# Gate and up projections of a GEGLU block as pairs of 64-row half tiles, with the weights loaded in chunks of 64 rows

## Chip, core and metric

The kernel runs on one core of one Trainium2 chip. The metric is device time in microseconds (us), the median of three runs. Traces come from one more execution under the hardware profiler; its span, from the first to the last instruction, is a little shorter than its own time.

## What is computed

For x of 2048 tokens by 448 features, in bf16:

```python
xn = _layernorm(x)
out = x + attention(xn, wqkv, wo) + (gelu(xn @ w_gate) * (xn @ w_up)) @ w_down
# attention: 16 heads of 28, causal, each token sees itself and the 255 before it
# w_gate, w_up: 448 x 1792; w_down: 1792 x 448
```

## The kernel before

Tokens are worked in four blocks (`qb`) of 512. `xnT` holds the normalized x with features on the partitions: 448 features are three chunks of 128 and a rest of 64. The rest stands in chunk 3 twice, on partitions 0 to 63 and on 64 to 127, so that two 64-row matmuls can run side by side in the upper and lower half of the array.

TensorE (PE) executes in program order, and the program writes that order out by hand. A block has two stages.

`attention(qb, ...)` (from line 532) goes through score steps: 12 in block 0, 10 in the others. A step issues scores (line 616, tile shape 28 x 128 or 28 x 64), the exp on ScalarE (ACT, line 622) and, in some steps, PV (line 576). Between the steps, matmuls of other work are put in from a `Feed`, a queue of generators with a planned cost: `gen_qk` and `gen_v` (projections of this or the next block), `gen_up` (ups done early; three pairs in block 0, five in block 3) and `gen_down` (the output of the block before). A generator that yields `HOLD` has dense passes standing open, and its half passes are issued at the start of the next step.

`gated(qb, ...)` (lines 417 to 479) then computes gates and the ups that are left. There are 14 tiles of 128 FFN features, taken in pairs. Each output takes three dense passes of 128 rows (`three`, line 232 by the helper `mm3`) and one of 64 rows (`half`, line 238 by `mm_half`). The 64-row passes of several outputs are grouped, so that the array changes its tile shape less often: (0, 2), (4, 8, 6), (10, 12) in blocks 0 and 3, four groups in the others. ACT makes the gelu (line 464), VectorE (DVE) the product with the up (line 471, or 469 for an up done early). PV of the last four heads (`last_v`) stands behind the first group's halves. `hook` puts norms, transposes and the k3 copies of the next block in between.

PSUM has four banks for scores or gate pairs (`s`) and four more: `m` twice, `d` and `o`, given out by fixed tags.

Weights: `wu` and `wg` hold three chunks of 128 rows, each loaded by one DMA (lines 144 and 750). The rest of 64 rows is loaded to both halves, by tiles `wgu3` and `wug3` (lines 145, 146, 748, 749). All are issued from SyncE (SP): `wu` at the start, behind x and wqkv; `wg`, wo and wd in `loads()`, which `ahead3` calls in block 0's third step. x tiles 8 to 11 are loaded at line 147 (issued at 8.93 us), 12 to 15 at line 747 (22.96 us). `dma_transp` (line 217) transposes the normalized tiles 4 to 15 by DMA, also from SP. In block 0 the order of the feed is: projections of heads 4 to 15, two early ups, projections of block 1, one early up.

Of the kernel before, what the change touches and what calls it, by code (L numbers as in the profile page):

```python
# [8 lines left out]
ACT = mybir.ActivationFunctionType  # L9
# [7 lines left out]
P = 128  # L17
# [58 lines left out]
def kernel(  # L76
# [45 lines left out]
    def rows(w, c0, n):  # L122
        return w[c0 * P:(c0 + n) * P, :].rearrange("(c p) n -> p c n", p=P)

# [14 lines left out]

    ident = const.tile([P, P], bf16, name="ident")  # L140
# [3 lines left out]
    nc.sync.dma_start(out=wu[:, :, :], in_=rows(B_w_up, 0, 3))  # L144
# [36 lines left out]
    xnT = const.tile([P, 4, S], bf16, name="xnT")  # L181
    qT = const.tile([P, 4, S], bf16, name="qT")
# [59 lines left out]
    ring = [("m", "m", "d"), 0]  # L242

    def bank(name):

        tag = ring[0][ring[1] % len(ring[0])]
        ring[1] += 1
        return psum.tile([P, QB], f32, name=name, tag=tag, bufs=2 if tag == "m" else 1)
# [8 lines left out]
    def v_copy(t, pv, copy):  # L257
        copy(out=v_sb[:, t, :, 0:Dh], in_=pv.rearrange("p (h d) -> p h d", d=Dh))

    def gen_v(qb, ts):  # L260

        for t in ts:
            pvs = []
            for i in range(2):
                pvs.append(bank("pv")[:, 0:D])
# [17 lines left out]
    def qk_copies(qb, g, pq, pk):  # L283
        ts = slice(qb * QB, (qb + 1) * QB)
        nc.scalar.copy(out=qT[:, g, ts], in_=pq)
        nc.vector.tensor_copy(out=kT[:, g, ts], in_=pk)
        done.add((qb, g))

    def gen_qk(qb, gs, others=()):

        for g in gs:
            pq = bank("pq")[:, :]
            proj(pq, wqp, qb, g)
            if qb and g == 3:
# [4 lines left out]
                nc.scalar.copy(out=qT[:, 3, ts], in_=pq)  # L299
                done.add((qb, 3))  # L300
# [3 lines left out]
            pk = bank("pk")[:, :]  # L304
# [52 lines left out]
    UP1 = 1660  # L357
    STEP, PV = 450, 870

    hTs, oNs = {}, {}  # L360
    down_tag, last_tag, last_res = ["d"], [None], []

    def gen_down(qb, tags):

        hT, oN = hTs[qb], oNs[qb]
        for tt in range(4):
            t = 4 * qb + tt
            cs = slice(tt * P, (tt + 1) * P)
            for n, (lo, up) in enumerate(((0, D),) if t < NT - 1 else ((0, D // 2), (D // 2, D))):
                w = up - lo  # L370
                tag = tags[tt + n]
                down_tag[0] = tag
                po = psum.tile([P, QB], f32, name="po", tag=tag, bufs=2 if tag == "m" else 1)
# [11 lines left out]
                nc.vector.tensor_tensor(out=res[:, 0:w], in0=po[:, 0:w], in1=x_sb[:, t, lo:up], op=ALU.add)  # L385
                nc.sync.dma_start(out=outv[:, t, lo:up], in_=res[:, 0:w])
# [7 lines left out]
    def half(ps, f, gate, hi, ts, start, stop, m=P):  # L394

        w3 = wgu3 if gate != bool(hi) else wug3
        mm_half(ps, w3[:, f * P:(f + 1) * P], xnT[:, 3, ts], hi, start, stop, m)

    def three(ps, f, gate, ts, start, stop):
        w = wg if gate else wu  # L400
        mm3(ps, lambda c: w[:, c, f * P:(f + 1) * P], lambda c: xnT[:, c, ts], start, stop)

    def gen_up(qb, fs):

        ts = slice(qb * QB, (qb + 1) * QB)
        for f in fs:
            us = []
            for i in range(2):
                us.append(bank("ue"))
                three(us[i][:, :], f + i, False, ts, True, False)  # L410
                yield (650, HOLD) if i else 650
            for i in range(2):
                half(us[i][:, :], f + i, False, i, ts, False, True)
            for i in range(2):
                nc.vector.tensor_copy(out=hTs[qb][:, f + i, :], in_=us[i][:, :])  # L415
            yield -360

    def gated(qb, early, last_v, flush, hook):

        ts = slice(qb * QB, (qb + 1) * QB)  # L420
        hT = hTs[qb]
        turn = ["o" if down_tag[0] == "d" else "d", down_tag[0]] * 4

        def single(name, tag):
            return psum.tile([P, QB], f32, name=name, tag=tag, bufs=2 if tag == "m" else 1)[:, :]

        def begin(f, apart=False):
            last_tag[0] = turn[0] if f not in early else last_tag[0]
            pr = dict(f=f, us=[])
            if apart:  # L430
                pr["gs"] = [single("g0", tag) for tag in ("m", turn.pop(0))]
                return pr
            pr["gt"] = phase[0].pool.tile([P, 2, QB], f32, name="gt", tag="s")
            pr["gs"] = [pr["gt"][:, i, :] for i in range(2)]
            if f not in early:
                tags = ("m", turn.pop(0))
                if qb == 0 and f == 0:
                    tags = [ring[0][(ring[1] + i) % 3] for i in range(2)]
                    if "d" in tags:
                        turn.insert(0, "o")  # L440
                pr["us"] = [single("u0", tag) for tag in tags]
            return pr

        def dense(pr, start):
            f = pr["f"]
            gs = [(g, f + i, True) for i, g in enumerate(pr["gs"])]
            us = [(u, f + i, False) for i, u in enumerate(pr["us"])]
            for ps, fi, gate in (gs + us if f else us + gs):
                three(ps, fi, gate, ts, start, not start)

        def halves(pr, start, m):
            f = pr["f"]
            for i in range(2):
                if pr["us"]:
                    half(pr["gs"][i], f + i, True, 0, ts, start, not start, m)
                    half(pr["us"][i], f + i, False, 1, ts, start, not start, m)
                else:
                    half(pr["gs"][i], f + i, True, i, ts, start, not start, m)

        def end(pr):  # L460
            f = pr["f"]
            ge = work.tile([P, 2, QB], bf16, name="ge", bufs=2)
            if "gt" in pr:
                nc.scalar.activation(out=ge[:, :, :], in_=pr["gt"][:, :, :], func=ACT.Gelu_apprx_tanh)  # L464
            else:
                for i, g in enumerate(pr["gs"]):
                    nc.scalar.activation(out=ge[:, i, :], in_=g, func=ACT.Gelu_apprx_tanh)
            if not pr["us"]:
                nc.vector.tensor_tensor(out=hT[:, f:f + 2, :], in0=ge[:, :, :], in1=hT[:, f:f + 2, :], op=ALU.mult)
            for i, u in enumerate(pr["us"]):  # L470
                nc.vector.tensor_tensor(out=hT[:, f + i, :], in0=ge[:, i, :], in1=u, op=ALU.mult)  # L471
                flush()
            hook(f)

        for fs in ((0, 2), (4, 8, 6), (10, 12)) if qb in (0, 3) else ((0,), (2, 4), (6, 8), (10, 12)):
            prs = [begin(fs[0])]
            dense(prs[0], True)
            prs += [begin(f, len(fs) == 3 and f == fs[1]) for f in fs[1:]]
            for pr in prs:
                halves(pr, pr is not prs[0], 32 if qb and not fs[0] else P)  # L480
            if not fs[0]:
                last_v()
            end(prs[0])
            for pr in prs[1:]:
                dense(pr, False)
                end(pr)
# [49 lines left out]
    def attention(qb, feeds, aux, plan):  # L536
# [22 lines left out]
        def add_halves(oc, ov):  # L559
            nc.scalar.copy(out=oc[:, :], in_=ov[0][:, :])  # L560
            nc.vector.tensor_tensor(out=oc[:, :], in0=oc[:, :], in1=ov[1][:, :], op=ALU.add)  # L561

# [4 lines left out]
        def pv(g):  # L567

            tags = ("o",) if not qb else ("m", "m" if g < 3 else down_tag[0])
            ov = [psum.tile([P, QB], f32, name="ov", tag=tag, bufs=2 if tag == "m" else 1) for tag in tags]  # L570
            todo = parts.pop(g)
            for n, (half, kt, q0, nq, col, p_sb) in enumerate(todo):
                k0 = 64 * half if half else 0
                r = slice(k0, k0 + (P if half is None else 64))
                for j in range(4):
                    nc.tensor.matmul(ov[half or 0][32 * j:32 * j + 32, q0:q0 + nq], lhsT=v_sb[r, kt, 4 * g + j, :],  # L576
                                     rhs=p_sb[r, j, col:col + nq], start=n == (half or 0), stop=n + len(tags) >= len(todo),
                                     tile_position=(k0, 32 * j), skip_group_check=True)
            oc = work.tile([P, QB], f32, name="oc", tag="wb" if qb and g % 2 else "wa", bufs=1)
            if qb:  # L580
                if g == 2 or qb == NB - 1 and g == 3:
# [3 lines left out]
            else:  # L585
                nc.vector.tensor_copy(out=oc[:, :], in_=ov[0][:, :])
            copied.append((g, oc))

        if qb:
            feeds[0].run()  # L590
        steps = list(steps_of(qb))
        pvs = {4: 0, 6: 1, 9: 2} if qb else {4: 0, 7: 1, 10: 2}
        for i, (scores, ncol, edges) in enumerate(steps):
# [42 lines left out]
            else:  # L636
# [9 lines left out]
                share(feeds, want, to)  # L646
# [29 lines left out]
    def alone(name, tag):  # L676
        return psum.tile([P, QB], f32, name=name, tag=tag, bufs=1)[:, 0:D]

# [272 lines left out]
```

## Time and profile before

| | |
|---|---|
| median of 3 runs | 220.48 us (220.33 to 220.51) |
| profiled execution: its time | 221.15 us |
| profiled execution: span | 219.4 us |
| mean granted PE clock | 0.996 |
| DVE busy, ACT busy | 152.1 us, 133.3 us |
| 128-row passes of gates, ups and early ups (line 232) | 37.5 + 29.2 + 12.0 us in three groups |
| wu and wg, one DMA of 1,344 KB each | issued at 7.22 and 24.77 us |

The page gives busy times, and slices of the span in which a row of digits or of GB/s tells what went on when. In a group's line the numbers are busy time and mean length of one. Matmuls are pipelined: a pass of 512 columns is listed with 379 ns, and the next starts 216 ns after it. So starts are compared, not lengths. PEld is PE's loading of weights, which runs beside matmuls.

### The profile page before, as it was taken

To read this page: it belongs to the slowest core of one execution; us is meant where nothing else is said; L and a number is where in the kernel's file an instruction comes from. 1 tells how busy PE (TensorE), PEld (TensorE's weight loads), DVE (VectorE), ACT (ScalarE), POOL (GpSimd) and SP (SyncE) were. 2 spreads that over 40 slices of the span, in tenths; PEclk is the share of its full clock that TensorE was granted. 3 is DMA by queue.
4 is the path that set the end of the run, shared out by engine and by line. 5 is a ranking of instruction groups with operands and counts; after the bars stand their busy time and mean duration, and the time that the engine had idled before them with its cause. 6 is when DMAs were issued, how large, how long until landed. Compare 5 with 4: busy or idle time off the path is not lost.

```text
span 219.4 us, 5447 instructions
## 1 busy us (share of the span) xinstructions
PE 213.9 (98%) x2287; PEld 96.1 (44%) x2287; DVE 152.1 (69%) x346; ACT 133.3 (61%) x131; POOL 46.9 (21%) x80
## 2 busy tenths in 40 slices
PE   7999999999999999999999999999999999999993
PEld 2433333434444454444444445444344445444562
DVE  6787896799666883679565795386356799479521
ACT  3588788662878875432878888233486777565000
POOL 5377987320000120022000022022000022022001
PEclk9999999999999999999999999999999999999998
DMA  6993799104200001102300000200000000000011
GB/s 193 310 311 71 188 325 302 30 4 72 45 3 21 24 24 27 20 3 46 60 13 24 23 1 24 52 13 0 0 3 21 25 3 24 24 1 0 22 35 37
DMA packets 18045, 13.30 MB, mean 61 GB/s; under 512 B 8704, under 2 KB 16992, under 8 KB 18016
## 3 DMA queue, kind: packets, MB, share of 16 engines
q1 hardware_dynamic: 17072, 12.62, 21.1%
q8 instruction: 19, 0.31, 0.6%
q10 hardware_dynamic: 944, 0.29, 0.5%
q14 instruction: 10, 0.08, 0.1%
HBM read 9.15 MB, written 2.18 MB: 52 GB/s over the span
## 4 chain that ended last, share of the span: by engine, by line
PE 96%; ACT 1%; DVE 1%; issue 1%; DVEq 0%
PE po L380 20%; PE gt L232 16%; PE u L232 12%; PE sc L616 6%; PE po L375 6%; PE gt L238 5%; PE ue L232 5%; PE ov L576 5%; PE pq L232 4%; PE pv L232 4%; PE pk L232 3%; PE wps L191 2%; PE pq L238 1%; PE g L232 1%; PE ue L238 1%; PE pv L238 1%
## 5 line engine op out<-in xcount | busy, mean ns | idle before, releaser
L622 ACT ACTIVATE p_sb<-sc 128x2048 bf16<-128x2048 f32 (+2 forms) x42 | 73.8, 1758 | 12.6 <-PE sc L616 8.2
L380 PE MATMUL po<-wd,hT 128*128 128x448 bf16 (+1 forms) x238 | 49.8, 342 | 0.0
L464 ACT ACTIVATE ge<-gt 128x1024 bf16<-128x1024 f32 x26 | 26.6, 1024 | 34.9 <-PE u L238 20.1
L542 POOL TENSOR_TENSOR oN<-oc,l 128x512 bf16<-128x512 f32 x12 | 16.0, 1334 | 137.8 <-DVE l L556 87.4
L232 PE MATMUL gt<-xnT,wg 128*128 128x512 bf16 x156 | 37.5, 380 | 0.0
L471 DVE TENSOR_TENSOR hT<-ge,u 128x512 bf16<-128x512 bf16 x40 | 25.7, 682 | 12.9 <-ACT ge L464 12.9
L380 PEld LDWEIGHTS <-hT 128*128 128x128 bf16 x238 | 21.5, 98 | 18.8 <-issue 2.6
L232 PE MATMUL u<-xnT,wu 128*128 128x512 bf16 x120 | 29.2, 379 | 0.0
L523 DVE TENSOR_TENSOR p_sb<-p_sb,masks 128x256 bf16<-128x256 bf16 (+1 forms) x90 | 26.8, 353 | 0.4 <-ACT p_sb L622 0.4
L232 PEld LDWEIGHTS <-wg 128*128 128x128 bf16 x168 | 15.3, 98 | 21.3 <-issue 4.5
L232 PEld LDWEIGHTS <-wu 128*128 128x128 bf16 x168 | 16.0, 98 | 19.2 <-issue 1.0
L561 DVE TENSOR_TENSOR oc<-oc,ov 128x512 f32<-128x512 f32 x12 | 8.2, 687 | 16.5 <-ACT oc L560 16.5
L616 PE MATMUL sc<-qT,kT 28*64 28x320 bf16 (+7 forms) x640 | 16.9, 263 | 0.2
L415 DVE CAST hT<-ue 128x512 bf16<-128x512 f32 x16 | 10.2, 681 | 8.4 <-PE ue L238 8.3
L375 PE MATMUL po<-wo,oN 128*128 128x448 bf16 (+1 forms) x68 | 15.9, 343 | 0.0
L385 DVE TENSOR_TENSOR res<-po,x_sb 128x448 bf16<-128x448 f32 (+1 forms) x17 | 10.0, 586 | 8.6 <-PE po L380 8.4
L533 POOL TENSOR_SCALAR_AFFINE_SELECT p_sb<-p_sb 128x512 bf16<-128x512 bf16 (+1 forms) x20 | 14.2, 730 | 5.0 <-ACT p_sb L622 4.8
L238 PE MATMUL gt<-xnT,wgu 64*128 64x512 bf16 (+1 forms) x67 | 12.7, 380 | 0.0
L560 ACT COPY oc<-ov 128x512 f32<-128x512 f32 x12 | 7.0, 583 | 8.8 <-PE ov L576 8.8
L232 PE MATMUL pq<-xnT,wqp 128*128 128x512 bf16 x45 | 12.2, 380 | 0.1
L548 DVE STREAM_TRANSPOSE l<-oc 128x512 f32<-128x512 f32 x16 | 11.3, 704 | 1.4 <-POOL oN L542 1.2
L232 PE MATMUL ue<-xnT,wu 128*128 128x512 bf16 x48 | 12.0, 380 | 0.0
(97 smaller groups left out, 241.9 us busy)
## 6 DMA issues: line engine op xcount, KB each, us to landing
out_dram<-res SPq DMA_DIRECT2D x15, 112.0 KB
x_sb<-in_A_x_dram SPq DMA_DIRECT2D x3, 448.0 KB
wu<-in_B_w_up_dram SPq DMA_DIRECT2D x1, 1344.0 KB
wg<-in_B_w_gate_dram SPq DMA_DIRECT2D x1, 1344.0 KB
wd<-in_B_w_down_dram SPq DMA_DIRECT2D x3, 448.0 KB
wraw<-in_A_wqkv_dram SPq DMA_DIRECT2D x2, 252.0 KB
wo<-in_A_wo_dram SPq DMA_DIRECT2D x4, 98.0 KB
wv<-in_A_wqkv_dram SPq DMA_DIRECT2D x1, 336.0 KB
```

Of the source, the lines that this page charges most:

```text
L232: nc.tensor.matmul(ps, lhsT=lhs(c), rhs=rhs(c), start=start and c == 0, stop=stop and c == 2, skip_group_check=True)
L238: nc.tensor.matmul(ps[c:c + m], lhsT=lhs[p0:p0 + 64, c:c + m], rhs=rhs[p0:p0 + 64], start=start, stop=stop, tile_position=(p0, c), skip_gr ...
L375: nc.tensor.matmul(po[:, 0:w], lhsT=oN[:, g, cs], rhs=wo[:, g, lo:up], start=(g == 0), stop=False, skip_group_check=True)
L380: nc.tensor.matmul(po[:, 0:w], lhsT=hT[:, f, cs], rhs=wd[:, f, lo:up], start=False, stop=(f == NF - 1), skip_group_check=True)
L464: nc.scalar.activation(out=ge[:, :, :], in_=pr["gt"][:, :, :], func=ACT.Gelu_apprx_tanh)
L471: nc.vector.tensor_tensor(out=hT[:, f + i, :], in0=ge[:, i, :], in1=u, op=ALU.mult)
L523: nc.vector.tensor_tensor(out=reg, in0=reg, in1=m, op=ALU.mult)
L533: nc.gpsimd.affine_select(out=reg, in_=reg, pattern=mid + [[1 if diag else -1, min(w, P)]], compare_op=ALU.is_ge, fill=0.0, base=0 if diag ...
L542: nc.gpsimd.tensor_tensor(out=oN[:, g, :], in0=oc[:, :], in1=inv, op=ALU.mult)
L548: nc.vector.transpose(out=l1[:, :, :].rearrange("p a b -> p (a b)"), in_=oc[:, :])
L616: nc.tensor.matmul(ss[k0:k0 + nk, j, col:col + nq], lhsT=kT[r, g, kt * P + k0:kt * P + k0 + nk], rhs=qT[r, g, qb * QB + q0:qb * QB + q0 + ...
L622: nc.scalar.activation(out=p_sb[:, :, 0:ncol], in_=ss[:, :, 0:ncol], func=ACT.Exp, scale=SCALE)
```

## The change

All 448 rows of gate and up are cut in seven chunks of 64 (`c`). Partitions 0 to 63 of `wu` and `wg` hold a chunk's columns for FFN tiles 0 to 6, partitions 64 to 127 those for tiles 7 to 13. One pair `p` is the tiles p and p + 7: seven passes of 64 rows for each, side by side in the two halves of the array, into two PSUM banks. Each half needs all seven x chunks on its own partitions. Half of them stand there in `xnT`; for the others `xsw`, a copy of the block's three full chunks with the halves exchanged, is made by two DMAs (`swap`), in block 0 from ACT's queue, later from SP's at the start of the attention.

`wu` and `wg` are loaded by seven DMAs each (`load_ffn`), one per chunk. `wgu3` and `wug3` go. x tiles 8 to 11 are loaded in `loads()`, ahead of 12 to 15. The fixed PSUM tags give way to a list of four free banks: `take` hands out the one free longest, `give` puts it back where its last reader is issued. `gated` has no groups any more. The feed of block 0 mixes ups and projections, and the attention no longer starts with a run of `feeds[0]`.

```diff
-    wg = const.tile([P, 3, F], bf16, name="wg")
-    wu = const.tile([P, 3, F], bf16, name="wu")
-    wgu3 = const.tile([P, F], bf16, name="wgu3")
-    wug3 = const.tile([P, F], bf16, name="wug3")
+    wg = const.tile([P, 7, F // 2], bf16, name="wg")
+    wu = const.tile([P, 7, F // 2], bf16, name="wu")
...
+    def load_ffn(dst, w):
+        for c in range(7):
+            nc.sync.dma_start(out=dst[:, c, :], in_=w[64 * c:64 * c + 64, :].rearrange("p (h n) -> h p n", h=2))
...
+    load_ffn(wu, B_w_up)
...
-    nc.sync.dma_start(out=wu[:, :, :], in_=rows(B_w_up, 0, 3))
-    nc.sync.dma_start(out=wug3[0:64, :], in_=B_w_up[384:448, :])
-    nc.sync.dma_start(out=wgu3[64:128, :], in_=B_w_up[384:448, :])
-    nc.sync.dma_start(out=x_sb[:, 8:12, :], in_=xv[:, 8:12, :])
...
+    spare = ["b0", "b1", "b2", "b3"]
+    held = {}
+
+    def take(name, cols=QB, tag=None):
+        tag = tag or spare[0]
+        spare.remove(tag)
+        ps = psum.tile([P, QB], f32, name=name, tag=tag, bufs=1)[:, 0:cols]
+        held[id(ps)] = tag, ps
+        return ps
+
+    def give(*tiles):
+        for ps in tiles:
+            spare.append(held.pop(id(ps))[0])
...
+    def swap(qb, queue):
         ts = slice(qb * QB, (qb + 1) * QB)
+        for hi in range(2):
+            queue.dma_start(out=xsw[64 * hi:64 * hi + 64, :, :], in_=xnT[64 - 64 * hi:P - 64 * hi, 0:3, ts])
+
+    def chunk(pair, w, p, qb, c):
+        for hi, ps in enumerate(pair):
+            r = slice(64 * hi, 64 * hi + 64)
+            ts = slice(qb * QB, (qb + 1) * QB)
+            x = xnT[r, 3, ts] if c == 6 else xnT[r, c // 2, ts] if c % 2 == hi else xsw[r, c // 2, :]
+            nc.tensor.matmul(ps, lhsT=w[r, c, p * P:(p + 1) * P], rhs=x, start=c == 0, stop=c == 6,
+                             tile_position=(64 * hi, 0), skip_group_check=True)
...
+    def gen_up(qb, ps):
+        for p in ps:
+            us = [take("ue") for _ in range(2)]
+            for c in range(7):
+                chunk(us, wu, p, qb, c)
+                if c == 2:
+                    yield 640
+                if c == 5:
+                    yield 640, HOLD
...
+        up(0)
+        gate(0)
+        end(0)
+        gate(1)
...
+        for p in range(3, 7):
+            gate(p)
+            up(p)
+            end(p)
...
-                if g == 2 or qb == NB - 1 and g == 3:
+                if g > 1:
                     behind.append((oc, ov))
...
-        if qb:
-            feeds[0].run()
...
+                if qb == NB - 1:
+                    share(feeds[:1], want, 0)
+                    share(feeds, 0, to)
+                else:
+                    share(feeds, want, to)
...
     transp(3, nc.vector.tensor_copy, "b3")
+    swap(0, nc.scalar)
...
     def loads():
-        nc.sync.dma_start(out=x_sb[:, 12:16, :], in_=xv[:, 12:16, :])
-        nc.sync.dma_start(out=wgu3[0:64, :], in_=B_w_gate[384:448, :])
-        nc.sync.dma_start(out=wug3[64:128, :], in_=B_w_gate[384:448, :])
-        nc.sync.dma_start(out=wg[:, :, :], in_=rows(B_w_gate, 0, 3))
+        for t in (8, 12):
+            nc.sync.dma_start(out=x_sb[:, t:t + 4, :], in_=xv[:, t:t + 4, :])
+        load_ffn(wg, B_w_gate)
...
-            early = (2, 4, 8)
+            early = (1, 2, 4)
             feeds = [Feed((gen_qk(0, (1, 2, 3), [(t, pvs[t]) for t in (2, 3)]), 3 * QK1 + 360),
-                          (gen_up(0, (2, 8)), 2 * UP1), (gen_proj(1), PROJ), (gen_up(0, (4,)), UP1))]
+                          (gen_up(0, (1,)), UP1), (gen_v(1, (4,)), 1500), (gen_up(0, (4,)), UP1), (gen_v(1, (6,)), 1500),
+                          (gen_up(0, (2,)), UP1), (gen_qk(1, range(4)), PROJ - 3000))]
...
+        if qb:
+            swap(qb, nc.sync)
```

More of the change, by code (lines that the diff above doesn't have):

```diff
@@ L181 @@
     xnT = const.tile([P, 4, S], bf16, name="xnT")
+    xsw = const.tile([P, 3, QB], bf16, name="xsw")
     qT = const.tile([P, 4, S], bf16, name="qT")
@@ L258, in v_copy @@
         copy(out=v_sb[:, t, :, 0:Dh], in_=pv.rearrange("p (h d) -> p h d", d=Dh))
+        give(pv)
     def gen_v(qb, ts):
@@ L264, in gen_v @@
             for i in range(2):
-                pvs.append(bank("pv")[:, 0:D])
+                pvs.append(take("pv", D))
                 v_dense(t + i, pvs[i])
@@ L286, in qk_copies @@
         nc.vector.tensor_copy(out=kT[:, g, ts], in_=pk)
+        if not (qb == 0 and g == 0):
+            give(pq, pk)
         done.add((qb, g))
@@ L291, in gen_qk @@
         for g in gs:
-            pq = bank("pq")[:, :]
+            pq = take("pq")
             proj(pq, wqp, qb, g)
@@ L299, in gen_qk @@
                 nc.scalar.copy(out=qT[:, 3, ts], in_=pq)
+                give(pq)
                 done.add((qb, 3))
@@ L303, in gen_qk @@
             yield 650
-            pk = bank("pk")[:, :]
+            pk = take("pk")
             proj(pk, wkp, qb, g)
@@ L368, in gen_down @@
             cs = slice(tt * P, (tt + 1) * P)
[L369 removed]
+            for lo, up in ((0, D),) if t < NT - 1 else ((0, D // 2), (D // 2, D)):
                 w = up - lo
[L371 to L373 removed]
+                po = take("po")
                 for g in range(4):
@@ L418, in gated @@
+    def gen_up(qb, ps):
[7 more added lines that the diff above has]
+                    yield 640, HOLD
+            for i in range(2):
+                nc.vector.tensor_copy(out=hTs[qb][:, p + 7 * i, :], in_=us[i])
+            give(*us)
+            yield -320
     def gated(qb, early, last_v, flush, hook):
-        ts = slice(qb * QB, (qb + 1) * QB)
@@ L421, in gated @@
         hT = hTs[qb]
[L422 to L464, printed above, removed]
-            else:
[L466 to L486, printed above, removed]
+        us, ges = {}, {}
@@ new lines, in up, with gate @@
+        def up(p):
+            if p in early:
+                return
+            us[p] = [take("u") for _ in range(2)]
+            for c in range(7):
+                chunk(us[p], wu, p, qb, c)
+        def gate(p):
+            gt = phase[0].pool.tile([P, 2, QB], f32, name="gt", tag="s")
+            for c in range(7):
+                chunk([gt[:, i, :] for i in range(2)], wg, p, qb, c)
+            if not p:
+                last_v()
+            ges[p] = work.tile([P, 2, QB], bf16, name="ge", bufs=2)
+            nc.scalar.activation(out=ges[p][:, :, :], in_=gt[:, :, :], func=ACT.Gelu_apprx_tanh)
@@ new lines, in end @@
+        def end(p):
+            ge = ges.pop(p)
+            if p in early:
+                nc.vector.tensor_tensor(out=both(hT, p), in0=ge[:, :, :], in1=both(hT, p), op=ALU.mult)
+            else:
+                for i, u in enumerate(us.pop(p)):
+                    nc.vector.tensor_tensor(out=hT[:, p + 7 * i, :], in0=ge[:, i, :], in1=u, op=ALU.mult)
+                    give(u)
+                    flush()
+            hook(2 * p)
+        up(0)
+        gate(0)
+        end(0)
+        gate(1)
@@ L488, in steps_of @@
+        if 1 in early:
+            end(1)
+            gate(2)
+            up(2)
+        else:
+            gate(2)
+            up(1)
+            end(1)
+            up(2)
+        end(2)
+        for p in range(3, 7):
+            gate(p)
+            up(p)
+            end(p)
     def steps_of(qb):
@@ L567, in pv @@
         def pv(g):
-            tags = ("o",) if not qb else ("m", "m" if g < 3 else down_tag[0])
-            ov = [psum.tile([P, QB], f32, name="ov", tag=tag, bufs=2 if tag == "m" else 1) for tag in tags]
+            ov = [take("ov") for _ in range(2 if qb else 1)]
             todo = parts.pop(g)
@@ L684 @@
     norm(0)
-    transp(0, nc.scalar.copy, "o")
+    transp(0, nc.scalar.copy, "b2")
     stat(2)
@@ L689 @@
     warmup(1)
-    transp(1, nc.scalar.copy, "d")
+    transp(1, nc.scalar.copy, "b3")
     stat(3)
     rstd(3, 1)
-    pvs = [bank("pv")[:, 0:D]]
+    pvs = [take("pv", D)]
     v_dense(0, pvs[0])
@@ L696 @@
     pads(nc.vector.tensor_copy, wqp, slice(0, 1))
-    transp(2, nc.scalar.copy, "o")
-    pvs.append(bank("pv")[:, 0:D])
+    transp(2, nc.scalar.copy, "b2")
+    pvs.append(take("pv", D))
     v_dense(1, pvs[1])
@@ L704 @@
     make_masks()
-    transp(3, nc.vector.tensor_copy, "d")
-    pvs.append(alone("pv", "o"))
+    transp(3, nc.vector.tensor_copy, "b3")
+    swap(0, nc.scalar)
+    pvs.append(take("pv", D, "b2"))
     v_dense(2, pvs[2])
@@ L721 @@
     pads(nc.vector.tensor_copy, wkp, slice(1, 2))
-    pvs.append(alone("pv", "d"))
+    pvs.append(take("pv", D, "b3"))
     v_dense(3, pvs[3])
-    ring[1] = 0
     for dst in (wqp, wkp):
@@ L839 @@
     with tc.If(n_ok < 1, preferred_fallthrough_block=True, label="general"):
-        general_path(tc, locals_=dict(x_sb=x_sb, xnT=xnT, qT=qT, kT=kT, v_sb=v_sb, wg=wg, wu=wu, wgu3=wgu3, wd=wd, wo=wo,
+        general_path(tc, locals_=dict(x_sb=x_sb, xnT=xnT, qT=qT, kT=kT, v_sb=v_sb, wg=wg, wu=wu, xsw=xsw, wd=wd, wo=wo,
                                       ident=ident, outv=outv))
@@ L862, in general_path @@
             ts = slice(qb * QB, (qb + 1) * QB)
+            for hi in range(2):
+                nc.sync.dma_start(out=L["xsw"][64 * hi:64 * hi + 64, :, :], in_=xnT[64 - 64 * hi:P - 64 * hi, 0:3, ts])
             for f in range(NF):
-                fs = slice(f * P, (f + 1) * P)
+                hi, p = divmod(f, 7)
+                r = slice(64 * hi, 64 * hi + 64)
                 pg = ps.tile([P, QB], f32, name="pg", tag="pg")
                 pu = ps.tile([P, QB], f32, name="pu", tag="pu")
-                for i, (dst, w) in enumerate(((pg, L["wg"]), (pu, L["wu"]))):
-                    for c in range(3):
-                        nc.tensor.matmul(dst[:, :], lhsT=w[:, c, fs], rhs=xnT[:, c, ts], start=(c == 0), stop=False)
-                    p0 = 64 * i
-                    nc.tensor.matmul(dst[:, :], lhsT=L["wgu3"][p0:p0 + 64, fs], rhs=xnT[p0:p0 + 64, 3, ts], start=False, stop=True,
-                                     tile_position=(p0, 0))
+                for dst, w in ((pg, L["wg"]), (pu, L["wu"])):
+                    for c in range(7):
+                        x = xnT[r, 3, ts] if c == 6 else xnT[r, c // 2, ts] if c % 2 == hi else L["xsw"][r, c // 2, :]
+                        nc.tensor.matmul(dst[:, :], lhsT=w[r, c, p * P:(p + 1) * P], rhs=x, start=(c == 0), stop=(c == 6),
+                                         tile_position=(64 * hi, 0))
                 ge = wk.tile([P, QB], bf16, name="gge")
```

51 lines of the change are left out of this document (15 added, 36 removed).

## Prediction

> **What bounds the kernel now.** I read the page first: TensorE (PE) is busy for 98% of the span, and the chain that ended last is PE for 96% of it. The groups by line then show no PE wait on data after the first 1.4 us. So, up to small gaps, the time is the sum of what PE issues, and a change counts by the PE work it adds or removes, or by a wait it gives to PE.
>
> ```profile
> span 219.4 us, 5447 instructions
> PE 213.9 (98%) x2287; PEld 96.1 (44%) x2287; DVE 152.1 (69%) x346; ACT 133.3 (61%) x131; POOL 46.9 (21%) x80
> ...
> GB/s 193 310 311 71 188 325 302 30 4 72 45 3 21 24 24 27 20 3 46 60 13 24 23 1 24 52 13 0 0 3 21 25 3 24 24 1 0 22 35 37
> ...
> PE 96%; ACT 1%; DVE 1%; issue 1%; DVEq 0%
> ```
>
> The GB/s row (40 slices of 5.5 us) shows two bursts of loading: to 16.5 us, and from 23 to 38 us. They hold all weights; the rest of the row is small.
>
> Second, the timeline, for the price of PE's own order and the dates by which weights are needed (columns: start, length, engine, line):
>
> ```profile
> 7.22 0.49 SPq L144 DMA_DIRECT2D wu<-in_B_w_up_dram  x1
> ...
> 19.49 1.47 PE L232 MATMUL ue<-xnT,wu 128*128 128x512 bf16 x6
> ...
> 20.89 0.39 PE L238 MATMUL ue<-xnT,wug 64*128 64x512 bf16 x1
> ```
>
> ```profile
> 39.06 1.46 PE L232 MATMUL gt<-xnT,wg 128*128 128x512 bf16 x6
> ...
> 40.46 0.39 PE L238 MATMUL u<-xnT,wgu 64*128 64x512 bf16 x1
> ...
> 40.68 0.38 PE L238 MATMUL u<-xnT,wgu 64*128 64x512 bf16 x1
> ...
> 40.90 0.38 PE L238 MATMUL gt<-xnT,wgu 64*128 64x512 bf16 x1
> ...
> 41.20 0.67 PE L576 MATMUL ov<-p_sb,v_sb 128*32 128x128 bf16 x16
> ```
>
> The up weights are first used at 19.5 us, the gate weights at 39.1. Two 64-row matmuls side by side start every 0.22 us (40.46, 40.68, 40.90), as often as one 128-row matmul. Where the array's tile shape changes, the next start comes after 0.30 us, not 0.22: over all 161 changes of shape in the trace 0.09 to 0.10 us each, plus 0.01 on the matmul after, so 0.105.
>
> Third, SyncE's (SP's) waits:
>
> ```profile
> SPq L756 <- DMA wg<-in_B_w_gate_dram: 3.2, 1, 3.2
> ```
>
> The last wd load waited 3.2 us for wg, issued eight DMAs earlier; the second load of line 138 waited in the same way for the one eight before it, which ACT had issued. So a DMA is issued only when the one eight places before it, on SP's or ACT's queue alike, has landed.
>
> **The change, part by part.**
>
> *Matmuls.* Per block of 512 columns before: 28 outputs of 3 dense passes, and 28 halves in 14 pairs, 98 passes of 0.216 us. After: 14 output pairs of 7 pair passes, 98 again. Saved: 0. The 84 further weight loads per block (98 ns each) lie beside running matmuls, as now. In before at most four pairs stand in a row; in longer rows a pair could cost anything from 0.216 to 0.43 (no overlap). I take 0.216, which every group of pairs shows.
>
> *Changes of tile shape.* I counted them in program order. Gated stages of the four blocks: 29 before. After, each has one entry and two for the last PV: 12. In block 0's attention each of three early ups stood as dense, halves, scores; it now has one shape: 3 fewer. Block 3's ups share their steps with the down matmuls: 0. So 20 x 0.105 = 2.1 us less, 1.8 of it behind the first gate pair.
>
> *PSUM list, gelus, multiplies, the down chunk no longer put ahead of the scores.* Same sizes and nearly same counts; ACT at 61% and DVE at 69% cover them. If a bank comes late, a DVE eviction of 0.68 us shows on PE: from 0 to 0.68 a time. I take 0.
>
> *xsw.* Two SBUF copies of 192 KB a block. Blocks 1 to 3 have a score step or more ahead of the first use: 0, or their landing if that cover goes (about 2 us). Block 0's stand on ACT's queue, in front of rstd and the qT copy that the first scores wait for. ACT idles there from 9.40 to 11.41 us, which hides two issues (1.05 for two at line 130) if nothing holds them.
>
> *x tiles 8 to 11* move to about 23 us. Their statistics come at 27.3; 448 KB at 324 GB/s (the saturated rate, 9 to 16 us) is 1.4 us. 0.
>
> *The weight DMAs* decide. How many DMA engines carry one? The trace has 1,360 four-byte packets on SP's queue, and these fit one closing packet per engine: 16 for a transfer of 128 or 64 rows, 14 for 28 rows (kT<-k: four leave 56), 4 for four rows (k<-qT, k<-kT: eight leave 32), 32 for a transpose. 28 rows go to 14 engines by two, not to 16: an engine takes whole steps of the outermost dimension. In every transfer of before both sides have the same outermost count. The new ones have 128 partitions on one side and two column halves on the other (h, then 64 rows). Bounds: 16 engines and 2. I take 2, because the DRAM side has only two whole outer steps, and four rows made four engines.
>
> The Trainium skill (DMA: Bandwidth & Descriptors, section "Why a DMA increments its semaphore by 16 and not by 1") says that the engine count is the largest number up to 16 that divides both sides' slowest dimension; the 4, 14 and 16 of this trace agree, for 2 against 128 it would give 2, and the sum then is the one below.
>
> Rate of one engine: packets of 896 bytes took 41 ns, of 3,584 bytes 140, so 1,792 bytes lie at 74 ns (24.2 GB/s). A chunk of 64 rows is 64 packets on each of the two engines: 4.74 us, seven 33.2. Bounds: 20.2 GB/s (324 over 16 engines) gives 5.68, the slope between the two packet sizes (27.2) gives 4.22.
>
> *Up weights.* Engines turn to wu at 9.07 (its first 3,584-byte packets in before); 33.2 for wu and 1.1 for xsw (24 packets of 46 ns per engine) end at 43.4. ACT's two xsw issues stand eight places behind chunks 1 and 2 and wait for them, until 23.3 on the rows above; qT, scores and exps queue behind, some 12 us. PE comes to its first early up at about 31 and waits for chunk 6 till 43.4: 22.5 us late against 20.89.
>
> *Gate weights.* The transpose of tile 7 stands eight places behind up chunk 6: issued at 43.4 for 1.2 us; then x 8 to 15 by 45.9, whose first packets come 1.9 us after their issue begins (7.22 to 9.07 above), at 46.5, and take 2 x 1.3 us per engine: 49.1. Then seven chunks: 82.3. PE needs the 17 us from 20.9 to 38 of before and is at the gates by about 61, so it waits again, and this wait swallows the first. Last gate pair at 82.4 against 40.9: 41.5 late. wo and wd follow within 6 us, and the first down matmuls, 18 us behind the gates, do not see them.
>
> *Clock.* After standing, PE starts slow: the first ten matmuls took 4.45 us, 0.43 each. Such a start costs 2.2 us; 0 to 4, I take 2.2.
>
> **Sum**, against the profiled execution: span 219.4, its time 221.15. 41.5 + 2.2 - 1.8 = 41.9, so 263.0; the median of the runs (220.48) lies 0.67 lower: **262**, rounded. With the two bounds of the rate over 14 chunks (-7.3 and +13.2): 255 to 275.
>
> **The rivals.**
>
> *All 16 engines carry the weights* (not slower). For it: 128 partitions, and every 128-row transfer here did so. Against: the whole-step rule above. Weights then land by about 16 and 34 us, both ahead of need, and PE has only the 2.1 us of shape changes: 220.48 - 2.1 = **218.4** (217.8 to 219.9). It decides as soon as chunk 6 of the gates lands before 39 us. The Trainium skill (same page, "Rules for kernel authors") advises one 128-partition transfer rather than two to partition halves, as those serialize; by that the new loads would gain, and this rival would hold. No transfer here shows that.
>
> *Sixteen engines, but banks come late.* PV's two banks, a down bank and a unit's two make five wishes on four banks, served in the order of release. Each late bank is 0.68 us of PE; three of them eat the 2.1. Three in each of three attentions is +6.1: 218.4 + 6.1 = **224.5** (220 to 227). Against: now PV and projections share two banks and PE does not wait.
>
> *Pairs do not overlap in long rows:* 392 x up to 0.21 = up to +84 us. Against: every group here.
>
> **Chances.** Two engines 0.60; sixteen and the gain 0.27; sixteen and late banks 0.11 (0.01 faster, 0.05 same, 0.05 slower); long rows 0.02. A measurement of this kernel tells about 0.2% from no change. Faster 0.28, same 0.05, slower 0.67. The likeliest case alone spans 255 to 275. As the second case holds over 0.2, the range must reach it: 217.8 to 272, leaving out the slow end of the first.
>
> **What would show it.** Two engines: the DMA row at one or two tenths with about 45 GB/s from 9 to 80 us, four-byte packets fewer by 14 x 14; PE standing before the early up's last chunks and at the gates to about 82; behind that all as before, 2 us shorter. Sixteen: GB/s bursts as now, no PE wait, and starts 0.216 apart through the gated stages. Late banks: PE waits on DVE evictions at pv, po, pq and ue. Wrong at once: wg landing before 39 us, or 64-row pairs over 0.22 apart.

## The result, and the profile after

The changed kernel takes 263.11 us (median of six runs, 262.22 to 263.41), the kernel before beside it 220.50 us (six runs, 220.31 to 220.99). The ratio is 1.1925, 95% interval 1.1902 to 1.1947: slower by 42.6 us. The profiled execution took 263.41 us, with a span of 261.7 us and a mean granted PE clock of 0.915; against the profiled execution of before it is 42.26 us longer.

The page, with the same rows as shown of before: the span and the busy times, then PE, granted clock and GB/s in 40 slices (6.54 us each here), and the chain that ended last.

```profile
span 261.7 us, 6056 instructions
PE 220.0 (84%) x2572; PEld 98.3 (38%) x2581; DVE 152.1 (58%) x346; ACT 133.0 (51%) x129; POOL 47.3 (18%) x80
...
PE   7819303999013999999999999999999999999994
...
PEclk9967755699855899999999999999999999999999
...
GB/s 188 191 77 54 51 72 102 160 53 51 51 157 191 47 48 96 26 23 8 41 18 21 56 85 20 20 18 30 27 3 11 70 3 21 20 20 1 3 38 40
...
PE 67%; SPq 21%; DMA 9%; issue 1%; ACTq 0%; DVE 0%; DVEq 0%
```

PE's share has fallen from 98% to 84% of a longer span, but the time that it is busy has only gone from 213.9 to 220.0 us. So PE got little more work; it stands. The GB/s row says during what: two plateaus of 51 to 54 GB/s (slices 4 and 5, then 9 to 11), where before bursts of 300 GB/s and more brought the weights. The digit row of PE has its holes at the end of each plateau (slices 5 to 7 and 11 to 13), and behind slice 13 it is full, as it is throughout in the kernel before:

```profile
PE   7999999999999999999999999999999999999993
```

The chain gives SP's queue and the DMAs 30%.

Now PE's waits on DMAs (columns: us in total, times, the longest):

```profile
PE gt L424 <- DMA wg<-in_B_w_gate_dram: 15.6, 4, 5.0
PE ue L424 <- DMA wu<-in_B_w_up_dram: 14.4, 4, 4.0
PE sc L624 <- ACT qT L299: 5.9, 1, 5.9
```

Three waits, 35.9 us together: for the chunks of the gates, for the chunks of the ups, and one of the first scores for ACT. In the timeline each chunk's first pair stands behind its chunk; these are the first up pair's last chunk, the first gate pair's last two chunks, and the PV behind it (start, length, engine, line; in brackets the idle time before, and what ended it).

```profile
43.96 0.61 PE L424 MATMUL ue<-xnT,wu 64*128 64x512 bf16 x2 [3.96 <-DMA wu<-in_B_w_up_dram]
```

```profile
77.65 0.61 PE L424 MATMUL gt<-xsw,wg 64*128 64x512 bf16 x1 [5.04 <-DMA wg<-in_B_w_gate_dram]
...
82.83 0.61 PE L424 MATMUL gt<-xnT,wg 64*128 64x512 bf16 x2 [4.58 <-DMA wg<-in_B_w_gate_dram]
83.37 1.15 PE L585 MATMUL ov<-p_sb,v_sb 128*32 128x128 bf16 x16
```

The PV starts at 83.37 us, before at 41.20: 42.2 us late. From there to the end of the span it is 178.3 us, before 178.2. So all of the loss lies ahead of the first gate pair's end, and none behind it. The table by stage shows it again, first the last stage of the kernel before, then the changed kernel (from, to, length, busy time of PE, PEld, DVE, ACT and POOL with counts, granted clock, DMA share, GB/s):

```profile
41.20:219.40 178.20, 174.49 (x2012) 80.97 (x2010) 119.51 (x268) 103.06 (x88) 18.74 (x16) 1.00 0.09 21
...
16.50:44.00 27.50, 11.20 (x63) 3.32 (x63) 6.07 (x14) 9.49 (x13) 8.60 (x19) 0.62 0.42 64
44.00:63.30 19.30, 19.19 (x160) 7.23 (x162) 14.98 (x29) 13.22 (x15) 11.51 (x18) 0.85 0.36 105
63.30:83.40 20.10, 4.52 (x33) 1.33 (x36) 1.24 (x3) 2.32 (x3) 1.93 (x3) 0.67 0.40 119
83.40:261.70 178.30, 174.29 (x2272) 82.02 (x2276) 119.17 (x268) 102.86 (x86) 18.00 (x15) 0.99 0.13 32
```

PE is busy in 11.2 of 27.5 us while the ups arrive, then fully for 19.3 us with the work that had queued up, then in 4.5 of 20.1 us while the gates arrive.

### The profile page after: what moved, and what is told of

Its sections match the earlier page's. It is cut to its first block, busy times and chain, and to the rows that moved or that the text cites. A ratio compares the mean times of both kernels' runs of the same rounds, so it can differ in the third digit from the quotient of the medians.

```text
span 261.7 us, 6056 instructions
## 1 busy us (share of the span) xinstructions
PE 220.0 (84%) x2572; PEld 98.3 (38%) x2581; DVE 152.1 (58%) x346; ACT 133.0 (51%) x129; POOL 47.3 (18%) x80
## 3 DMA queue, kind: packets, MB, share of 16 engines
q10 hardware_dynamic: 1360, 0.68, 1.1%
## 4 chain that ended last, share of the span: by engine, by line
PE 67%; SPq 21%; DMA 9%; issue 1%; ACTq 0%; DVE 0%; DVEq 0%
PE po L395 17%; PE gt L424 17%; SPq L128 16%; PE u L424 11%; DMA wg<-in_B_w_gate_dram 7%; PE po L390 5%; PE sc L624 4%; PE ov L585 3%; PE ue L424 3%; SPq L220 3%; SPq L176 2%; DMA wraw<-in_A_wqkv_dram 2%; PE pq L235 2%; PE pv L235 2%; PE pk L235 1%
## 5 line engine op out<-in xcount | busy, mean ns | idle before, releaser
L424 PE MATMUL gt<-xnT,wg 64*128 64x512 bf16 x224 | 48.0, 388 | 8.7 <-DMA wg<-in_B_w_gate_dram 8.7
L424 PE MATMUL gt<-xsw,wg 64*128 64x512 bf16 x168 | 42.9, 388 | 6.8 <-DMA wg<-in_B_w_gate_dram 6.8
L424 PEld LDWEIGHTS <-wg 64*128 64x128 bf16 x392 | 19.0, 96 | 41.0 <-DMA wg<-in_B_w_gate_dram 17.4
L424 PEld LDWEIGHTS <-wu 64*128 64x128 bf16 x392 | 18.8, 94 | 40.2 <-DMA wu<-in_B_w_up_dram 16.4
L424 PE MATMUL u<-xnT,wu 64*128 64x512 bf16 x160 | 33.2, 376 | 0.0
L424 PE MATMUL u<-xsw,wu 64*128 64x512 bf16 x120 | 29.1, 376 | 0.0
L424 PE MATMUL ue<-xnT,wu 64*128 64x512 bf16 x64 | 15.4, 400 | 7.9 <-DMA wu<-in_B_w_up_dram 7.9
L424 PE MATMUL ue<-xsw,wu 64*128 64x512 bf16 x48 | 13.0, 398 | 6.5 <-DMA wu<-in_B_w_up_dram 6.5
L390 PE MATMUL po<-wo,oN 128*128 128x448 bf16 (+1 forms) x68 | 15.6, 343 | 0.0
L624 PEld LDWEIGHTS <-kT 28*64 28x64 bf16 (+1 forms) x640 | 7.7, 102 | 18.0 <-issue 16.5
L595 DVE COPY oc<-ov 128x512 f32<-128x512 f32 x4 | 2.7, 687 | 20.0 <-PE ov L585 20.0
```

The source lines that it names most:

```text
L390: nc.tensor.matmul(po[:, 0:w], lhsT=oN[:, g, cs], rhs=wo[:, g, lo:up], start=(g == 0), stop=False, skip_group_check=True)
L424: nc.tensor.matmul(ps, lhsT=w[r, c, p * P:(p + 1) * P], rhs=x, start=c == 0, stop=c == 6, tile_position=(64 * hi, 0), skip_group_check=True)
L624: nc.tensor.matmul(ss[k0:k0 + nk, j, col:col + nq], lhsT=kT[r, g, kt * P + k0:kt * P + k0 + nk], rhs=qT[r, g, qb * QB + q0:qb * QB + q0 + ...
```

## The experiments

The theory is that of the prediction: each of the new loads is carried by two DMA engines of sixteen, since its DRAM side has only two outermost steps, and nothing else in the change costs much. The rivals: the pairs, the banks or the feed cost time of their own, or it is the number of the loads and not their form. Each experiment ran beside runs of the kernel before on the same chip; these gave medians of 220.63 to 220.78 us.

**The same kernel with loads of 64 partitions.** Two DMAs for each weight, one for each half of the partitions, so that 64 rows are the outermost dimension on both sides:

```diff
-        for c in range(7):
-            nc.sync.dma_start(out=dst[:, c, :], in_=w[64 * c:64 * c + 64, :].rearrange("p (h n) -> h p n", h=2))
+        for h in range(2):
+            nc.sync.dma_start(out=dst[64 * h:64 * h + 64, :, :],
+                              in_=w[:, h * (F // 2):(h + 1) * (F // 2)].rearrange("(c p) n -> p c n", p=64))
```

> The changed kernel with one edit: each of the two weights comes by two DMAs of 64 partitions (one per column half, all seven chunks in it) instead of seven of 128 partitions, so that both sides have 64 outermost steps. Bytes, packets of 1,792 bytes and tile layout stay. Theory (two engines carry each of the seven): now 16 engines carry them, the weights land by about 16 and 34 us as in the kernel before, no wait of PE on a weight is left, and what remains is the 2.1 us of shape changes: 218.4 us (217.8 to 219.9). Rival (the packets of 1,792 bytes or the two column halves are slow by themselves): still 250 us or more. Rival (sixteen engines, but the four banks come late): 224.5 us (220 to 227), with PE waits on DVE evictions.

Measured: 219.36 us, 0.9953 of before (0.9939 to 0.9967), and 43.7 us below the changed kernel. The page:

```profile
PE 211.7 (97%) x2572; PEld 97.8 (45%) x2581; DVE 151.6 (70%) x346; ACT 132.9 (61%) x129; POOL 46.8 (22%) x80
...
GB/s 189 266 223 150 205 240 234 229 4 72 74 48 24 24 19 31 21 0 52 70 75 21 24 3 21 56 14 0 0 75 21 5 24 24 21 5 0 25 23 47
```

and the whole of PE's waits:

```profile
PE wps L195 <- DVE wo L171: 1.4, 1, 1.4
```

The two plateaus are gone, and PE waits for no weight and no bank. SP's queue ends its transfers with 1,424 four-byte packets, by which the prediction counts engines, against 1,388 in the changed kernel: sixteen for each of the four loads, in place of two for each of the fourteen. Everything else of the change is still there, pairs, `xsw`, the list of banks, the late x tiles, and it is worth a gain of about 1 us. So the form of the loads is the whole loss. The bursts do not reach the 300 GB/s of before, though: a packet of 1,792 bytes took 142 ns here in the median, 74 in the changed kernel. This I had not expected; it comes back in the last section.

**The same with as many small loads.** Two DMAs for each chunk, 14 for each weight:

```diff
+            for h in range(2):
+                nc.sync.dma_start(out=dst[64 * h:64 * h + 64, c, :], in_=w[64 * c:64 * c + 64, h * (F // 2):(h + 1) * (F // 2)])
```

> The changed kernel with fourteen DMAs per weight, one for each chunk and column half, each of 64 partitions and 64 rows: same packets, twice the issues. Theory (engines per transfer): 16 engines each, weights on time, and only the issues cost, 14 x 0.6 us on SP and the two xsw copies on ACT held until the DMA eight places before them, an up chunk, has landed at about 14 us: 218.4 plus 0 to 3, so 220 us (218 to 222). Rival (many issues and the rule of eight places make the 42 us, not the engines): as slow as the changed kernel or slower, 263 us or more.

Measured: 219.81 us, 0.9954 (0.9936 to 0.9972). So neither small loads nor many of them are the cost. The one wait of PE that is new, `PE sc L625 <- ACT qT L300` in the list of waits, lasts 1.3 us: with 14 issues in the queue ACT's first work is late, but by little. Here the median packet took 74 ns again, but the mean is 102 ns (133 with two loads), and the ups land no earlier: at 18.4 us, with two loads at 17.8.

**One weight at a time.** Seven two-engine loads for the gates alone (`if w is B_w_up:` the two loads of above, else the seven), and for the ups alone:

> Up weights by two DMAs of 64 partitions each, gate weights by the seven of the change. Theory: no wait at the early ups; gate chunks start about 27.5 us and take 7 x 4.58 and the longer first, 33 us: the last gate pair at 60.6 instead of 40.9 us, 19.7 late, and PE starts slow once, which about pays for the shape changes: 240 us (236 to 245). Rival (only the early start matters, where ACT and the up wait meet): about 219 us.

> Gate weights by two DMAs of 64 partitions each, up weights by the seven of the change. Theory: the last early up chunk lands at 43.5 us as in the changed kernel, PE is 22.7 us late there against the kernel before, the gate weights are there by 56 us, ahead of the gates at 63: 220.5 + 22.7 + 2.2 - 2.1 = 243 us (239 to 247). Rival (only the gate weights hold the end, the first wait is swallowed in any case): about 219 us.

Measured: 242.12 us for the gates alone, 1.0976 (1.0943 to 1.1010), +21.5 us; 244.22 us for the ups alone, 1.1071 (1.1052 to 1.1091), +23.6 us. PE's waits for the one and the other:

```profile
PE gt L429 <- DMA wg<-in_B_w_gate_dram: 19.2, 5, 4.5
...
PE ue L429 <- DMA xsw<-xnT: 0.6, 1, 0.6
```

```profile
PE ue L429 <- DMA wu<-in_B_w_up_dram: 15.2, 4, 4.1
PE sc L629 <- ACT qT L304: 6.0, 1, 6.0
```

Either weight alone costs about half of the loss: gates that are loaded from 27.4 to 61.3 us instead of in a burst hold PE until 61.84 us, and the ups' wait brings the same 6.0 us at the first scores as in the changed kernel. Against the two-load kernel that is +22.8 and +24.9 us, 47.6 together, where both in one kernel cost 43.7. The date of the PV behind the first gate pair shows where the difference lies: 41.0 us with two loads for each weight, 62.4 with seven for the gates alone, 66.2 with seven for the ups alone, 83.4 with seven for both. The ups alone make PE 25.2 us later there, but beside the seven loads of the gates they move the end of these only from 61.3 to 81.9 us, by 20.6. The rest of their delay lies under the gates' wait.

**The rule by itself.** The kernel before, with four DMAs of 224 KB from SP ahead of the last down matmuls, when `wu` is no longer read; they serve no computation. Outermost on the DRAM side are 2, 4, 8 and 16 column parts, on the SBUF side always 64 partitions or more:

```diff
+    for h, c, lo in ((2, 0, 0), (4, 0, 896), (8, 1, 0), (16, 1, 512)):
+        nc.sync.dma_start(out=wu[:, c, lo:lo + F // h], in_=B_w_up[0:P // h, :].rearrange("p (h n) -> h p n", h=h))
```

> The kernel before, with four more DMAs issued from SP ahead of the last down matmuls, into the up weights when these are no longer read (they serve no computation): from B_w_up, with 2, 4, 8 and 16 column pieces as the outermost step on the DRAM side and 128 partitions on the other; 224, 112, 56 and 28 KB in packets of 1,792, 896, 448 and 224 bytes. Theory (an engine takes whole outermost steps): they run on 2, 4, 8 and 16 engines, end in so many four-byte packets, 30 in all, and take about 4.6, 1.3, 0.4 and 0.1 us of packets. Rival (any transfer into 128 partitions takes 16 engines): 64 four-byte packets, each transfer under 0.8 us. Time about as before.

Measured: 1,390 four-byte packets on SP's queue, 30 more than the 1,360 of before: 2 + 4 + 8 + 16. So a transfer goes to as many engines as the DRAM side has outermost steps, though its other side has 128 partitions. (Sixteen engines for each would have been 64 more.) The packets of the first one lie between 189.7 and 195.5 us: 5.8 us for what two engines carry in 4.6 when alone. The other three end by 197.2 us, so their own times can't be read here. The single time, 220.76 us, is that of before: at that place nothing waits for them. The Trainium skill (DMA: Bandwidth & Descriptors, section "Why a DMA increments its semaphore by 16 and not by 1") has the engine count as the largest number up to 16 that divides the outermost sizes of both sides; the sum of the four counts agrees.

**The price of a change of tile shape.** The kernel before with every gated pair in a group of its own, which adds 28 changes and nothing else that I knew of:

```diff
-        for fs in ((0, 2), (4, 8, 6), (10, 12)) if qb in (0, 3) else ((0,), (2, 4), (6, 8), (10, 12)):
+        for fs in ((0,), (2,), (4,), (6,), (8,), (10,), (12,)):
```

> The kernel before with one edit: in the gated stage every pair of FFN tiles is a group of its own (seven groups of one pair in each block, in place of three or four), so that the array changes its tile shape 28 times more; the passes stay the same. Theory (each change of shape costs 0.105 us of time on PE): +2.9 us, 223.5 us (223.0 to 224.2). Rival (the two-load version gained less than 2.1 us because changes of shape cost only half as much in time as their starts show): +1.5 us, 222.1 us.

Measured: 226.61 us, 1.0263 (1.0247 to 1.0280), +5.8 us. Both numbers missed it. In the trace there are 189 changes, 28 more. What the starts behind a change lose over the 0.216 us of a pass of 512 columns (less in proportion for fewer) sums to 19.31 us, before 16.45, when the three long waits of the next line are left out: +2.9 us, or 0.10 each, as the theory has it. But the edit also did something that I had not seen:

```profile
PE sc L616 <- ACT ge L464: 2.0, 3, 0.7
```

The last group is now a single pair, so its gelu ends a step later, and the first scores of the next block wait for the PSUM that it reads: 0.7 us at the end of three of the gated stages. That seems to leave some 0.9 us of the 5.8. In the traces, though, a middle block grows by 1.51 us, from 51.48 to 52.99, and nothing of this is left over: six changes take 0.60, the first scores start 0.74 later for the gelu, and scores behind a projection start 0.16 later, released by an exp. The price of a change stands by the trace; the time alone can't confirm it.

**What the rest of the change is worth.** The kernel before, unchanged, and the two-load kernel once more:

> The kernel before, unchanged, for a second profile and for what a comparison of equal kernels gives. The profiled execution of before took 221.15 us, 0.67 over its median, that of the two-load version 219.11, 0.25 under its. Theory (the shape changes are worth about 2 us in every execution): a second profile of before has the same length from score to score, and the difference of the medians is short of 2 us by something behind or ahead of PE's chain. Rival (the profiled execution of before was long by chance, inside the blocks): its blocks of scores are shorter by some tenths each. The ratio of equal kernels should be 1.000 within 0.002.

> The version with two DMAs per weight once more, beside the kernel before on the same chip. Theory: 1.0 to 2.1 us less than before, 218.5 to 219.5 us, no PE wait on a weight. Rival (its gain of 0.5% was chance): within 0.2% of before.

Measured: the kernel before 220.82 us, 1.0002 (0.9993 to 1.0012); two loads 219.60 us, 0.9947 (0.9933 to 0.9961). The gain is there a second time: 1.2 us. The second profile of the kernel before has a block of 51.48 us from scores to scores, as the first, and the two-load kernel one of 50.89: 0.6 us in each middle block, which is their five shape changes fewer (0.12 each). Part of the gain is lost at the first early up:

```profile
19.99 0.39 PE L425 MATMUL ue<-xsw,wu 64*128 64x512 bf16 x2 [0.19 <-DMA xsw<-xnT]
```

`xsw` lands after its first reader is ready, since it shares the engines with the slow packets of `wu`; the pair starts at 19.99 us, some 0.4 us late. The last block gives no gain either: from its first scores to the end it takes 60.2 us in the kernel before and 60.4 with two loads, and these runs don't show why.

**A version that keeps the gain.** Six loads of 64 partitions for each weight, the halves in turn, and w3k ahead of them:

```diff
+        for lo, up in ((0, 3), (3, 5), (5, 7)):
+            for h in range(2):
+                nc.sync.dma_start(out=dst[64 * h:64 * h + 64, lo:up, :],
+                                  in_=w[64 * lo:64 * up, h * (F // 2):(h + 1) * (F // 2)].rearrange("(c p) n -> p c n", p=64))
```

> The changed kernel with six DMAs per weight, each of 64 partitions, for the chunks 0 to 2, 3 to 4 and 5 to 6, the two column halves in turn, and with the small w3k loads issued ahead of the up weights. In both profiles of the two-load version packets of 1,792 bytes took 142 ns instead of 74 and the first xsw copy landed at 19.0 us or later, in one of them with PE 0.36 us late at the first early up. Theory (transfers into one half of the partitions hold each other up, and halves in turn do not): packets near 74 ns, up weights by 16 us, xsw by 15.5 us, no stall at the first early up, no wait of the first scores on ACT: 219.0 us (218.5 to 219.5), 0.1 to 0.5 less than the two-load version. Rival (packets into 64 partitions are slow in any order): 142 ns again and a time as with two loads, 219.4 to 219.6.

Measured: 219.04 us (six runs, 218.34 to 219.33), 0.9912 of before (0.9895 to 0.9929): 1.7 us faster than the kernel before, the best of all. But two of its reasons missed. The packets took 125 ns in the median (a tenth of them 74 or less), not 74 throughout, and `xsw` landed at 18.1 us, not 15.5. That was still in time: PE has no wait at the first early up. The gates' loading takes 7.5 us (27.3 to 34.8), with two loads 8.2, so the order of the halves brings back only part of the rate. The edit also moves w3k, and the runs don't tell the two apart in the gain.

## Why the prediction was right, step by step

- **Two engines: right.** Outermost steps set the number, shown by the 30 closing packets and by the kernels with two and with fourteen loads, which change only the weights' loads: they take 43.7 and 43.3 us off. In the changed kernel there are 1,388 such packets: 1,360, less 96 for the six weight loads on sixteen engines that went, plus 28 for fourteen on two, plus 96 for six `xsw` copies. The prediction's "fewer by 14 x 14" compared the new loads with sixteen engines; against the trace of before it was the wrong number to look for.
- **Rate: right.** Packets of 74 ns, as interpolated. The first chunks land at 15.6, 20.2 and 25.2 us; most steps are 4.5 to 4.6 us against 4.74. The first took 6.2 (from 9.4 us), the third 5.0, the last two of the gates 5.3 and 5.1. That the seven ups still end on the date of the sum is partly luck: long steps and short ones cancel.
- **Up weights: right in time, wrong in one wait.** They ended at 43.5 us (predicted 43.4), and the early up's last pair is 23.1 us late (22.5). But ACT's wait was half of what I had: the second `xsw` issue was held for chunk 0, until 16.45 us, not for chunks 1 and 2 until 23.3, because ACT issued it ahead of w3k and I had counted it behind. First scores 5.6 us late, not some 12; first early up at 26.8 us, not 31. The wait for the chunks swallows either.

ACT's queue in the timeline, and what stood behind it:

```profile
16.45 0.60 ACTq L414 DMA_DIRECT2D xsw<-xnT  x1
```

```profile
18.16 0.61 PE L624 MATMUL sc<-qT,kT 28*128 28x128 bf16 x8 [5.89 <-ACT qT L299]
```

- **Gate weights: right.** Landed at 81.9 us against 82.3, the last pair 41.9 us late (42.2 at the PV) against 41.5. It starts 0.9 us behind the landing of its chunk, where I had 0.1. PE came to the gated stage at 63.3 and to its first gate at 64.8, not 61. The way there was another, though. I let the transpose of tile 7 wait eight places behind chunk 6. In the trace SP itself stands: its issues of `wu` alone take 22.43 us for seven, w3k comes at 30.3, and the four transposes stand behind it.

```profile
7.85 22.43 SPq L128 DMA_DIRECT2D wu<-in_B_w_up_dram  x7
30.32 6.57 SPq L176 DMA_DIRECT2D w3k<-in_A_wqkv_dram  x2
37.01 6.99 SPq L220 DMA_TRANSPOSE xnT<-xn  x4
44.05 1.12 SPq L757 DMA_DIRECT2D x_sb<-in_A_x_dram  x2
```

Either way the transposes are through when the ups are, at 44 us (43.4 predicted), so the dates agree.
- **Clock: 1.9 for 2.2 us.** The page has the clock at half for much of the waits, and the pairs behind the first PV still start 0.43 us apart, then 0.216:

```profile
85.29 1.05 PE L424 MATMUL gt<-xsw,wg 64*128 64x512 bf16 x2
85.72 1.05 PE L424 MATMUL gt<-xnT,wg 64*128 64x512 bf16 x2
86.14 1.05 PE L424 MATMUL gt<-xsw,wg 64*128 64x512 bf16 x2
...
88.88 0.59 PE L424 MATMUL gt<-xsw,wg 64*128 64x512 bf16 x2
89.10 0.59 PE L424 MATMUL gt<-xnT,wg 64*128 64x512 bf16 x2
```

From 84.46 to 87.37 us that loses about 1.4 us, and the PV's 1.15 us for 0.67 another 0.5. Against the two-load kernel, which has no such wait, the changed one is 2.0 us longer behind this PV (178.3 and 176.3 us). PE starts slow three times here; the first two times lie ahead of a longer wait and so cost nothing.
- **Changes of shape: 19 fewer, not 20.** The trace has 142 for 161: in the gated stages 13 for 30 (I had 12 for 29), in block 0's attention 35 for 37 (I had three fewer). At 0.10 us that is 1.9 us for 2.1. In the changed kernel the 1.7 of it behind the first gate pair and the 1.9 of the clock nearly cancel, so the 178 us behind are the same. In the kernels with quick loads the measured gain is 1.2 us (two loads) and 1.7 (six), less than the 2.1 forecast for quick loads.
- **Costed at nothing, and nothing: passes, banks, x tiles.** In the kernels with this change PE waits for a late bank once, 0.2 us in the one with slow ups alone, and long rows of pairs start 0.216 us apart, so both those rivals fall. `xsw` cost 0.4 us in one execution of the two-load kernel, and 0.6 in the one with slow gates alone.
- **The sum** of 41.9 us was 42.26; by the parts measured here it is 41.9 + 1.9 - 1.7 = 42.1. Two misses, on ACT's wait and on SP's queue, did not show, as a longer wait lay over both: that was luck. The range reached from a gain to a loss of 50 us and says little; what held is the case that had a chance of 0.60, and its sum.

## What to carry to other kernels

Count the outermost steps of both sides of a DMA before you count its bytes: 128 partitions on one side helped nothing while the other had two column halves, and cost 43 us. If a view must be split in halves, issue one load for each half of the partitions, and look at GB/s in the slices. A loading burst that has become a plateau is seen there at once, and what it costs is the date of the last chunk less the date at which it was used before, not its share of busy time.

## What the runs showed of the hardware that was not expected

- Loads to 64 partitions use sixteen engines (the 1,424 closing packets above), but an engine carries them at about half its rate: 142 ns in the median for a packet of 1,792 bytes against 74, and 238 GB/s in all from 9 to 16 us against 322 in the kernel before. The kernel before shows the same, without column halves: from 13.3 to 15.4 us, while its two loads of the rest of 64 rows run, the rate is 239 GB/s and a packet of 3,584 bytes takes 229 ns in the median, against 140 for `wu` just before. With the halves as alternating small loads the median is 74 ns (14 loads) and 125 (six), the mean 102 and 122. The Trainium skill states such a rate (SBUF — State Buffer, section "Door 1: The DMA port swizzle (why `[64,N]` ≈ `[32,N]`)"): partitions 0 to 63 reach only 8 of 16 ports, 196 GB/s against 328; the runs agree on the rate, as the two-load kernel's gates, 1,568 KB, take 8.2 us, 197 GB/s. It also advises one transfer of 128 partitions over two to partition halves (DMA: Bandwidth & Descriptors, section "Rules for kernel authors"). Here the two halves gained 43.7 us on the one, despite their slower packets, as the one had only two outermost steps.
- An issuing engine can be held inside its issue: SP for 22.43 us over seven, when their two engines were behind. No run here shows what holds it.
- The granted clock of the changed kernel stands at half from 15.6 to 22.5, from 29.3 to 49.8 and from 70.2 to 87.3 us. So it falls in waits of 1.8 to 5.9 us, with at most one chunk's matmuls between two of them, and PE still works at half speed for some 4 to 6 us after the last of each (from 18.2, 44.0 and 83.4 us).
